# One RWKV-7 recurrence and squared-ReLU FFN on one core: the square taken from PSUM, early parts moved up, a solve's input loaded ahead, and one more group by seven products

## The chip, the cores and the metric

The kernel runs on one core of a Trainium2 chip. The metric is the device time of one execution in microseconds (us). The engines are named as in the profile: PE (TensorE, matrix products and transposes), DVE (VectorE), ACT (ScalarE), POOL (GpSimd) and SP (SyncE, which issues most DMAs). The time before is a median of 948.04 us over 3 runs (943.51 to 949.66).

## The reference

```python
# 4 batches, 8 heads, 768 steps, head size 40, one 40x40 state per head
for t in range(S):
    y[:, :, t] = einsum('bhd,bhde->bhe', r_t, state)
    Sa = einsum('bhde,bhe->bhd', state, a_t)
    state = state * w_t[:, :, None, :] - einsum('bhd,bhe->bhde', Sa, b_t)
    state = state + einsum('bhd,bhe->bhde', v_t, k_t)
x = y as 3072 rows of 320                    # 8 heads x 40
out = maximum(x @ w_in, 0)**2 @ w_out        # w_in 320 x 2048, w_out 2048 x 320
```

All of it is fp32. The two weight matrices arrive as the bits of float64 numbers and are turned into fp32 on the chip.

## The kernel before

**Chunks.** Time is cut into 24 chunks of 128 steps (4 batches of 6), and a chunk holds all 8 heads. Two chunks make a group of 256 rows for the FFN, so there are 12 groups, 0 to 11.

**The early part** of a chunk (`early`) needs nothing of the state: it transposes w, takes running products of the decays by scans on DVE (L372 to L381), transposes b and a, scales them (`bT` L387, `decay` L388) and forms the matrix N, which is stored to HBM (`kept_d` for the later chunks). `ahead` says in which slot which chunk's early part is made.

**The solves** invert triangular matrices made of N. POOL does them, a unit of chunks at a time, by 63 steps of a product (L478) and a subtraction (L480). Units of sizes 4, 4 and 2 end the list: chunks 14 to 17 (I call it unit 8), 18 to 21 (unit 9), 22 and 23 (unit 10). `take` loads a unit's N into the one buffer `half_n` on POOL's own DMA queue (L451); the result `half_t` is stored to `kept_t` (L487), and a later slot loads its chunk's inverse `T` from there, on SP's queue (L507).

**A slot** is the time in which chunk i's chain runs (state, `minus_x`, `xr`, and last `tokens`, L697), with the next chunk's inputs prepared (products masked into `RV`, `A`, `RX` at L347; `kvT` L548; `in_k`, `in_b` L588), one or two early parts, and FFN work between them. Slots 0 to 6 are laid out by hand as a string of words: in it `pa`/`pd` are the two halves of a piece of weight conversion (ACT L275; DVE L284 to L292), `th` and `wh` the FFN calls below, `sq` the square. Slots 7 to 23 come from `sorted_slot`. Nothing is reordered at run time: each engine works through its instructions in the order of these calls.

**The FFN** (class `Ffn`). A quad is a quarter of the hidden rows of a group; a group has four. `thirds` opens two PSUM banks of the pool `ps_f` (which has only two) with 4 products, `whole` adds 8 more, and ACT writes the relu to `hid` (L762), one operation a bank. `square` later multiplies `hid` by itself on DVE (L769). `make_quarter` adds a quad's share to one chunk's output by 4 products of 128x320; from group `SEVEN` = 6 on, `make_piece` instead makes a group's output by seven sums of 8 products of 128x160 each (P1 to P7), with sums of weight blocks made once (`sum_weights`) and sums of `hid` blocks (L825, L826). The profile shows every fp32 product as two records, so a quarter is a row x8 and a piece a row x16. The names `in_ab`, `in_w` and `decay` in the rows of the pieces are buffers that hold sums of weights by then.

Of the kernel before, what the change touches and what calls it, by code (L numbers as in the profile page):

```python
# [17 lines left out]
def kernel(  # L18
# [22 lines left out]
    nc = tc.nc  # L41
# [682 lines left out]
    class Ffn:  # L724
# [26 lines left out]
        def whole(self):  # L751
# [4 lines left out]
            for e, p_ in enumerate(self.banks):  # L756
# [5 lines left out]
                nc.scalar.activation(h_, p_.rearrange("p f t -> p (f t)"), Act.Relu)  # L762
                self.unsquared.append(h_)
# [3 lines left out]
        def square(self):  # L767
            for h_ in self.unsquared:
                nc.vector.tensor_tensor(h_, h_, h_, Alu.mult)  # L769
            self.squared += len(self.unsquared) // 2  # L770
            self.unsquared = []
# [25 lines left out]
        def make_piece(self, g, at):  # L797


            names = "P1 P4 P2 P7 P6 P5 P3" if g == len(order) // GB - 1 else "P4 P1 P2 P7 P6 P5 P3"  # L800
# [11 lines left out]
            if at in (0, 3, 4):  # L812
                self.bank = psum(ps_f)
# [5 lines left out]
            for n in range(NF // 2):  # L819
                k, e, m_ = n // 4, n // 2 % 2, n % 2  # L820
                mm(ps[part], x_[:, n], seven[name][k * QF + 2 * m_ + e], at in (0, 3, 4) and n == 0)
# [14 lines left out]
            if at == 3:  # L836
                plus(hi1, ps[0], hi0)
            if at == 6:
                plus(hi0, ps[2], hi0)
                plus(hi1, ps[0], hi1)  # L840
                plus(hi0, ps[0], hi0)
                less(lo1, hi1, lo1)
                plus(hi0, ps[1], hi0)
                plus(hi1, ps[1], hi1)
                for n, o_ in enumerate(self.ends):
                    bb, c = order[g * GB + n]
                    row = bb * S + c * C
                    store(out[row:row + C, :], o_, 2)
# [14 lines left out]
    SEVEN = 6  # L863
# [169 lines left out]
    ahead = {7: (14, 15), 8: (16, 17)}  # L1033
    ahead.update({i: (i + 9,) for i in range(9, len(order) - 9)})

    done = set(range(14))
    unit = len(solves)
# [26 lines left out]
    def sorted_slot(i, g, ch):  # L1064
# [4 lines left out]
        one, two = (made + [iter(()), iter(())])[:2]  # L1069
# [7 lines left out]

        if more and "x" in n:
# [6 lines left out]
        step(of(turn_rv), on(one), on(one))  # L1085
        fetch_next(j + 1, "r")
        step(second.make_quarter)
        step(on(ch), of(decay_state))
        if i == 2 * SEVEN + 3:
            sum_weights(0)  # L1090
        if i == 2 * SEVEN + 4:
            sum_weights(3)
        step(of(make_rv), second.thirds)
        step(on(ch), on(one))
        if fine:
            join()
        step(second.whole)
        step(on(ch))
        step(on(one), of(turn_k))
        if i == 2 * SEVEN + 3:  # L1100
            sum_weights(1)
# [67 lines left out]
```

## Time and profile before

| | |
|---|---|
| median of 3 runs (us) | 948.04 (943.51 to 949.66) |
| the profiled execution (us) | 944.9, of which the span is 943.2 |
| mean granted PE clock | 0.956 |
| PE busy | 883.6 us (94%) |
| DVE busy | 518.8 us (55%) |
| ACT busy | 283.0 us (30%) |
| POOL busy | 525.1 us (56%) |

The span runs from the first to the last instruction; the execution has 1.7 us around it. Rows below that start with a time are from the timeline or the chain of waits: start and duration in us from the start of the span, engine, line, operation, output<-input, and in brackets the idle time of that engine just before and what ended it. xN says that N instructions of the same kind are merged into the row; for PE the duration of the last one overlaps the next row.

### The profile page before, as it was taken

Reading aid. Unit: us, or ns where it says so; the run is one execution under the profiler, and the core shown is the slowest. Engines: PE = TensorE matmul, PEld = TensorE weight load, DVE = VectorE, ACT = ScalarE, POOL = GpSimd, SP = SyncE. Lnnn points to the kernel's source line nnn. Section 1 sums busy time; section 2 is a strip of 40 time slices with the busy share of each in tenths; the row PEclk is TensorE's granted clock in tenths of the full one; section 3 lists DMA queues with packets and bytes.
Section 4 is the critical chain, followed back from the end, with each engine's and each line's share of the span. In section 5 each row is a group of like instructions: output and inputs, shape, how many; then the busy total and the mean of one; then the engine's idle time right before and its main releaser. Section 6 shows DMA issues by size and latency. Waiting matters only on the chain.

```text
span 943.2 us, 23218 instructions
## 1 busy us (share of the span) xinstructions
PE 883.6 (94%) x9404; PEld 738.8 (78%) x9404; DVE 518.8 (55%) x1209; ACT 283.0 (30%) x735; POOL 525.1 (56%) x935
## 2 busy tenths in 40 slices
PE   6678989889999999999999999999989999999997
PEld 5466657667787887888888888888978999988897
DVE  5827657888853454553755454675634645343243
ACT  3033334544523333333333332222212222222110
POOL 4557347065007786418999959999958986000000
PEclk9858988799899999999999999999998999999999
DMA  9769779766866578987665776604355445040000
GB/s 110 127 145 143 171 136 180 184 160 129 178 101 154 93 128 161 170 163 131 126 92 87 127 178 113 115 17 86 57 131 93 74 81 99 18 75 1 22 15 15
DMA packets 253269, 103.41 MB, mean 110 GB/s; under 512 B 234154, under 2 KB 240298, under 8 KB 252010
## 3 DMA queue, kind: packets, MB, share of 16 engines
q1 hardware_dynamic: 244709, 83.00, 49.7%
q0 software_dynamic: 3760, 17.10, 7.4%
q10 hardware_dynamic: 4693, 1.83, 0.9%
q8 instruction: 74, 1.21, 0.6%
q14 instruction: 33, 0.27, 0.1%
HBM read 69.00 MB, written 30.92 MB: 106 GB/s over the span
## 4 chain that ended last, share of the span: by engine, by line
PE 47%; POOL 25%; DVE 11%; DMA 8%; issue 4%; ACT 3%; SPq 2%; ACTq 0%; DVEq 0%; POOLq 0%
PE ps_f L87 21%; POOL half_t L480 13%; POOL half_p L478 12%; PE ps_w L87 11%; PE ps_c L87 8%; PE ps_w L331 3%; DMA half_n<-kept_d 2%; PE ps_f L264 2%; DMA in_r<-in_r_dram 1%; DMA T<-kept_t 1%; SPq L513 1%; DVE half_t L480 1%; DVE half_t L478 1%; DVE decay L381 1%; DMA dec<-kept_e 1%
## 5 line engine op out<-in xcount | busy, mean ns | idle before, releaser
L478 POOL TENSOR_TENSOR half_p<-half_n,half_t 128x462 f32<-128x462 f32 (+39 forms) x406 | 229.2, 565 | 75.7 <-DMA half_n<-kept_q 23.7
L480 POOL TENSOR_TENSOR half_t<-half_t,half_p 128x462 f32<-128x462 f32 (+39 forms) x406 | 245.7, 605 | 31.8
L87 PE MATMUL ps_f<-w_out,hid 128*128 128x320 f32 (+1 forms) x768 | 165.4, 368 | 0.0
L87 PE MATMUL ps_f<-tokens,w_in 128*128 128x256 f32 x672 | 157.0, 387 | 0.0
L87 PEld LDWEIGHTS ps_f<-w_out,hid 128*128 128x128 f32 x768 | 123.2, 190 | 26.0
L87 PEld LDWEIGHTS ps_f<-tokens,w_in 128*128 128x128 f32 x672 | 125.9, 192 | 19.1 <-issue 2.0
L769 DVE TENSOR_TENSOR hid<-hid 128x512 f32<-128x512 f32 x96 | 82.3, 899 | 10.3 <-ACT hid L762 9.9
L762 ACT ACTIVATE hid<-ps_f 128x512 f32<-128x512 f32 x84 | 49.8, 596 | 80.9 <-PE ps_f L87 80.8
L372 DVE TENSOR_TENSOR_SCAN decay<-ps_w,ones 128x64 f32<-128x64 f32 x88 | 23.9, 271 | 66.1 <-PE ps_w L331 66.0
L451 POOL DMA_DIRECT2D half_n<-kept_q x18 | 9.5, 534 | 88.7 <-DMA kept_m<-N 26.4
L697 DVE TENSOR_TENSOR tokens<-ps_c,dec 128x512 f32<-128x512 f32 x24 | 16.6, 691 | 72.9 <-PE ps_c L87 71.1
L347 DVE TENSOR_TENSOR RX<-ps_w,upper 128x512 f32<-128x512 f32 x48 | 30.8, 684 | 38.4 <-PE ps_w L87 38.2
L87 PEld LDWEIGHTS ps_c<-xr,T 64*64 64x64 f32 x768 | 29.7, 146 | 25.2 <-issue 18.4
L264 PE MATMUL ps_f<-ident 128*128 128x512 f32 (+3 forms) x108 | 49.4, 591 | 0.0
L87 PE MATMUL ps_f<-tokens,w_third 64*128 64x256 f32 x336 | 47.6, 394 | 0.1
L398 ACT COPY N<-ps_w 128x256 f32<-128x256 f32 x48 | 17.7, 369 | 94.9 <-PE ps_w L87 67.7
L548 DVE TENSOR_TENSOR kvT<-ps_w,dec 128x512 f32<-128x512 f32 x24 | 16.4, 684 | 52.5 <-PE ps_w L331 23.3
L87 PE MATMUL ps_c<-xr,T 64*64 64x40 f32 x768 | 35.7, 240 | 10.1 <-DMA T<-kept_t 5.4
L347 DVE TENSOR_TENSOR RV<-ps_w,upper 128x512 f32<-128x512 f32 x48 | 30.9, 685 | 21.2 <-PE ps_w L87 20.9
L658 ACT COPY minus_x<-ps_c 64x160 f32<-64x160 f32 x96 | 27.5, 287 | 36.5 <-PE ps_c L87 32.6
L331 PE MATMUL ps_w<-ident,in_ab 128*128 128x128 f32 x184 | 28.5, 301 | 10.1 <-DVE RV L347 8.1
L87 PE MATMUL ps_w<-rT,kvT 40*128 40x128 f32 x384 | 31.4, 308 | 5.4 <-ACT kvT L561 5.1
(167 smaller groups left out, 1548.9 us busy)
## 6 DMA issues: line engine op xcount, KB each, us to landing
dec<-kept_e SPq DMA_DIRECT2D x22, 633.8 KB
kept_e<-decay SPq DMA_DIRECT2D x19, 633.8 KB
in_w<-in_w_dram SPq DMA_DIRECT2D x24, 160.0 KB
in_b<-in_b_dram SPq DMA_DIRECT2D x24, 160.0 KB
in_ab<-in_a_dram SPq DMA_DIRECT2D x24, 160.0 KB
in_r<-in_r_dram SPq DMA_DIRECT2D x24, 160.0 KB
in_v<-in_v_dram SPq DMA_DIRECT2D x24, 160.0 KB
in_k<-in_k_dram SPq DMA_DIRECT2D x22, 160.0 KB
```

What stands on the lines that cost most here:

```text
L87: nc.tensor.matmul(o, l_, r_, start=start, stop=True, skip_group_check=True)
L264: nc.tensor.matmul(fill_bank[:, :n * 128], ident, ident.unsqueeze(1).to_broadcast([128, n, 128]), start=True, stop=True, skip_group_check= ...
L331: nc.tensor.transpose(p_[:, q * 128:(q + 1) * 128], pair(x_, q), ident)
L347: nc.vector.tensor_tensor(t_, p_, over4(upper), Alu.mult)
L372: nc.vector.tensor_tensor_scan(up[:, q, MID + 1:C + 1], wT[:, q, MID:], ones, 1.0, Alu.mult, Alu.mult)
L398: nc.scalar.copy(plain, p_[:, ::2].rearrange("s h (f t) -> s f h t", f=2))
L478: eng.tensor_tensor(p_, part[:, at:at + m_].unsqueeze(1).to_broadcast([128, n, m_]), t3[:, :n, s:s + 1].to_broadcast([128, n, m_]), Alu.mult)
L480: eng.tensor_tensor(t3[:, :n, s + 1:], t3[:, :n, s + 1:], p_, Alu.subtract)
L658: nc.scalar.copy(flipped(xn)[halves[half], flip, :, :, :D], by_pair(xs[halves[half ^ flip]]))
L697: nc.vector.tensor_tensor(t_, y_, g["up"][:, :, :C], Alu.mult)
L762: nc.scalar.activation(h_, p_.rearrange("p f t -> p (f t)"), Act.Relu)
L769: nc.vector.tensor_tensor(h_, h_, h_, Alu.mult)
```

## The change

Five things are changed.

1. `whole` issues, right behind the two relus, one DVE operation each that reads the PSUM bank and the relu: max(PSUM, 0) x relu, written over `hid`. `square` keeps only its count. The operation so stands in DVE's order at the place of `whole` (L763 in the changed kernel) and no longer at that of `square`, and a PSUM bank of `ps_f` comes free after it.
2. `SEVEN` is 5: group 5 (chunks 10 and 11) is also made by seven products, and the weight sums are made two slots earlier (slots 13 and 14).
3. In the last group, P6's and P5's sums are added before the last product, from banks of another pool, and one half of the output is stored earlier.
4. `ahead`: slot 9 also makes two early parts (chunks 18 and 19), and chunks 20 to 23 follow one slot earlier than before. The parts are now issued at numbered places of the slot.
5. `solve_more`: the first 2048 of the 3072 words a row of the next unit's N are loaded once the unit before has passed step 40, the rest when that unit has ended.

```diff
@@ -760,13 +760,12 @@
                         mm(p_[:, n], w_in[:, j, f * 128:(f + 1) * 128], t_[:, j, :], False)
                 h_ = hidden[:, self.place(k), e]
                 nc.scalar.activation(h_, p_.rearrange("p f t -> p (f t)"), Act.Relu)
+                nc.vector.scalar_tensor_tensor(h_, p_.rearrange("p f t -> p (f t)"), 0.0, h_, Alu.max, Alu.mult)
                 self.unsquared.append(h_)
             self.banks = None
             self.quad += 1
 
         def square(self):
-            for h_ in self.unsquared:
-                nc.vector.tensor_tensor(h_, h_, h_, Alu.mult)
             self.squared += len(self.unsquared) // 2
             self.unsquared = []
 
 
-            names = "P1 P4 P2 P7 P6 P5 P3" if g == len(order) // GB - 1 else "P4 P1 P2 P7 P6 P5 P3"
+            last = g == len(order) // GB - 1
+            names = "P1 P4 P2 P7 P6 P5 P3" if last or g == SEVEN else "P4 P1 P2 P7 P6 P5 P3"
...
             half, chunk = {"P1": (0, 0), "P2": (1, 0), "P4": (1, 1), "P7": (0, 1), "P6": (0, 0), "P5": (1, 1), "P3": (1, 0)}[name]
             part = {"P1": 0, "P2": 2, "P4": 1, "P7": 0, "P6": 0, "P5": 1, "P3": 2}[name]
-            if at in (0, 3, 4):
-                self.bank = psum(ps_f)
+            fresh = at in ((0, 3, 4, 5, 6) if last else (0, 3, 4))
...
-                mm(ps[part], x_[:, n], seven[name][k * QF + 2 * m_ + e], at in (0, 3, 4) and n == 0)
+                mm(ps[part], x_[:, n], seven[name][k * QF + 2 * m_ + e], fresh and n == 0)
...
+            if at == 4:
+                self.sixth = ps[0]
+            if at == (4 if last else 6):
+                plus(hi1, self.sixth, hi1)
+                plus(hi0, self.sixth, hi0)
+                less(lo1, hi1, lo1)
+            if at == 5:
+                self.fifth = ps[1]
+            if at == (5 if last else 6):
+                plus(hi1, self.fifth, hi1)
+                plus(hi0, self.fifth, hi0)
             if at == 6:
                 plus(hi0, ps[2], hi0)
-                plus(hi1, ps[0], hi1)
-                plus(hi0, ps[0], hi0)
-                less(lo1, hi1, lo1)
-                plus(hi0, ps[1], hi0)
-                plus(hi1, ps[1], hi1)
-                for n, o_ in enumerate(self.ends):
-                    bb, c = order[g * GB + n]
-                    row = bb * S + c * C
-                    store(out[row:row + C, :], o_, 2)
+            for n in {5: (1,), 6: (0,)}.get(at, ()) if last else (1, 0) if at == 6 else ():
+                bb, c = order[g * GB + n]
+                row = bb * S + c * C
+                store(out[row:row + C, :], self.ends[n], 2)
             return True
 
         def rest(self):
...
-    SEVEN = 6
+    SEVEN = 5
...
 
-    ahead = {7: (14, 15), 8: (16, 17)}
-    ahead.update({i: (i + 9,) for i in range(9, len(order) - 9)})
+    ahead = {7: (14, 15), 8: (16, 17), 9: (18, 19), 10: (20,), 11: (21,), 12: (22,), 13: (23,)}
 
     done = set(range(14))
-    unit = len(solves)
+    under_way = [len(solves), None]
+
+    def solve_more():
+
+        u, now = under_way
+        while u < len(units) and all(m_ in done for m_ in range(len(order)) if unit_of[m_] == u):
+            flush()
+            take(u, own, slice(0, EARLIER))
+            if now is not None:
+                run(now)
+            take(u, own, slice(EARLIER, None))
+            now = solving(u, (40,))
+            next(now)
+            u += 1
+        if u == len(units) and now is not None:
+            run(now)
+            now = None
+        under_way[:] = u, now
...
-        one, two = (made + [iter(()), iter(())])[:2]
+        place = [0]
+
+        def at_place():
+            place[0] += 1
+            for gen, places in zip(made, ((1, 1, 5, 8, 10, 12), (9, 10, 11, 12, 13, 14) if i == 8 else (13, 14, 14, 14, 14, 15))):
+                for _ in range(places.count(place[0])):
+                    next(gen, None)
+
...
+        def sums(n_):
+            if i == 2 * SEVEN + 3 + (n_ > 0):
+                sum_weights(n_)
+
...
             join()
-        step(of(turn_rv), on(one), on(one))
+        step(of(turn_rv), at_place)
         fetch_next(j + 1, "r")
-        step(second.make_quarter)
-        step(on(ch), of(decay_state))
-        if i == 2 * SEVEN + 3:
-            sum_weights(0)
-        if i == 2 * SEVEN + 4:
-            sum_weights(3)
-        step(of(make_rv), second.thirds)
-        step(on(ch), on(one))
+        step(second.make_quarter, at_place)
+        step(on(ch), of(decay_state), at_place)
+        sums(0)
+        sums(1)
+        step(of(make_rv), second.thirds, at_place)
+        step(on(ch), at_place)
         if fine:
             join()
-        step(second.whole)
-        step(on(ch))
-        step(on(one), of(turn_k))
-        if i == 2 * SEVEN + 3:
-            sum_weights(1)
-        step(of(turn_down))
-        step(on(one), on(ch))
-        step(on(ch), of(scale_kb))
+        step(second.whole, at_place)
+        sums(3)
...
+        step(on(ch), of(make_a), second.thirds, at_place)
         fetch_next(j + 1, "v")
-        step(of(turn_state), second.square, second.whole, on(two))
-        if i == 2 * SEVEN + 3:
-            sum_weights(2)
+        step(of(turn_state), second.square, second.whole, at_place)
+        sums(2)
         if not early_join and not fine:
             join()
...
-        step(second.square, second.make_quarter, on(two), on(two))
-        if i in ahead and len(ahead[i]) > 1:
-            step(on(two), on(two))
-        step(second.make_quarter, on(two))
-        for gen in (one, two, joining):
+        step(second.square, second.make_quarter, at_place)
+        step(second.make_quarter, at_place)
+        for gen in made + [joining]:
...
         ch = g["chain"]
+        sorted_slot(i, g, ch)
         done.update(ahead.get(i, ()))
-        sorted_slot(i, g, ch)
-        while unit < len(units) and all(m_ in done for m_ in range(len(order)) if unit_of[m_] == unit):
-            flush()
-            take(unit, own)
-            solve(unit)
-            unit += 1
+        solve_more()
```

What moves on the engines is shown at three places.

DVE, slot 4 of the part laid out by hand: the wholes of the first two quads of group 0, between the masked `RV` and the second half of the early part of chunk 8 (`decay_126`). L284 to L292 are a piece of weight conversion. Before:

```order
L347 TENSOR_TENSOR RV<-ps_w,upper 128x512 x2
L284 SCALAR_TENSOR_TENSOR hid<-hid 128x320
L285 SCALAR_TENSOR_TENSOR w_out<-w_out,hid 128x320
L290 TENSOR_SCALAR hid<-hid 128x320
L291 TENSOR_TENSOR w_out<-hid,w_out 128x320
L292 TENSOR_SCALAR hid<-hid 128x320
L377 RECIPROCAL decay_126<-decay_126 128x4
L378 RECIPROCAL decay_126<-decay_126 128x4
```

and after:

```order
L347 TENSOR_TENSOR RV<-ps_w,upper 128x512 x2
L763 SCALAR_TENSOR_TENSOR hid<-ps_f,hid 128x512 x2
L284 SCALAR_TENSOR_TENSOR hid<-hid 128x320
L285 SCALAR_TENSOR_TENSOR w_out<-w_out,hid 128x320
L290 TENSOR_SCALAR hid<-hid 128x320
L291 TENSOR_TENSOR w_out<-hid,w_out 128x320
L292 TENSOR_SCALAR hid<-hid 128x320
L763 SCALAR_TENSOR_TENSOR hid<-ps_f,hid 128x512 x2
L377 RECIPROCAL decay_126<-decay_126 128x4
L378 RECIPROCAL decay_126<-decay_126 128x4
```

Two pairs of squares now stand ahead of the reciprocals; before, all eight squares of this group stood behind the next masked `A`, further down.

DVE, slot 8, which makes a second early part (`decay_127`) as the next chunk's `in_k`, `in_b` and `RX` are prepared. Before:

```order
L387 TENSOR_TENSOR bT<-ps_w,decay_126 128x512
L388 TENSOR_TENSOR decay_126<-ps_w,decay_126 128x4x128
L588 TENSOR_TENSOR in_k_107<-ps_w,in_k_107 128x8x40
L588 TENSOR_TENSOR in_b_87<-ps_w,in_b_87 128x8x40
L347 TENSOR_TENSOR RX<-ps_w,upper 128x512 x2
```

and after (eight scans of `decay_127` stand between `decay` L388 and the first row, and six more behind the last):

```order
L373 SCALAR_TENSOR_TENSOR decay_127<-ps_w,ones 128x64
L588 TENSOR_TENSOR in_k_107<-ps_w,in_k_107 128x8x40
L588 TENSOR_TENSOR in_b_87<-ps_w,in_b_87 128x8x40
L377 RECIPROCAL decay_127<-decay_127 128x4
L378 RECIPROCAL decay_127<-decay_127 128x4
L380 SCALAR_TENSOR_TENSOR decay_127<-ps_w,decay_127,ones 128x63
L381 SCALAR_TENSOR_TENSOR decay_127<-ps_w,decay_127,ones 128x63
```

The sixteen scans and two reciprocals of the second early part come ahead of `RX`; before they came after `tokens`, at the end of the slot.

POOL, from step 40 of unit 8 on; `kept_d_220` is the N of unit 9. The difference at step 40:

```order
 L478 TENSOR_TENSOR half_p<-half_n,half_t 128x480
 L480 TENSOR_TENSOR half_t<-half_t,half_p 128x20x24
+L451 DMA half_n<-kept_d_220 64x2048 x2
 L478 TENSOR_TENSOR half_p<-half_n,half_t 128x483
 L480 TENSOR_TENSOR half_t<-half_t,half_p 128x21x23
```

and at the end of that unit:

```order
 L480 TENSOR_TENSOR half_t<-half_t,half_p 128x32
 L487 DMA kept_t_230<-half_t 128x2048
-L451 DMA half_n<-kept_d_220 64x3072 x2
+L451 DMA half_n<-kept_d_220 64x1024 x2
 L467 MEMSET half_t 128x2048
 L469 MEMSET half_t 64x32 x2
```

Two thirds of the load of unit 9 now stand ahead of the last 23 steps of unit 8. The load waits for the stores of chunks 18 to 21, and these 23 steps stand behind it on POOL.

More of the change, by code (lines that the diff above doesn't have):

```diff
@@ L811, in make_piece @@
             part = {"P1": 0, "P2": 2, "P4": 1, "P7": 0, "P6": 0, "P5": 1, "P3": 2}[name]
-            if at in (0, 3, 4):
-                self.bank = psum(ps_f)
+            fresh = at in ((0, 3, 4, 5, 6) if last else (0, 3, 4))
+            if fresh:
+                self.bank = psum(ps_w if at > 4 else ps_f)
             if at == 0:
@@ L1084, in sorted_slot @@
             join()
-        step(of(turn_rv), on(one), on(one))
+        step(of(turn_rv), at_place)
         fetch_next(j + 1, "r")
-        step(second.make_quarter)
-        step(on(ch), of(decay_state))
-        if i == 2 * SEVEN + 3:
-            sum_weights(0)
-        if i == 2 * SEVEN + 4:
-            sum_weights(3)
-        step(of(make_rv), second.thirds)
-        step(on(ch), on(one))
+        step(second.make_quarter, at_place)
[4 more added lines that the diff above has]
+        step(on(ch), at_place)
         if fine:
             join()
-        step(second.whole)
-        step(on(ch))
-        step(on(one), of(turn_k))
-        if i == 2 * SEVEN + 3:
-            sum_weights(1)
-        step(of(turn_down))
-        step(on(one), on(ch))
-        step(on(ch), of(scale_kb))
+        step(second.whole, at_place)
+        sums(3)
+        step(on(ch), at_place)
+        step(at_place, of(turn_k))
+        step(of(turn_down), at_place)
+        step(at_place, on(ch))
+        step(on(ch), of(scale_kb), at_place)
         if fine:
             join()
-        step(on(ch), of(make_a), second.thirds, on(one))
+        step(on(ch), of(make_a), second.thirds, at_place)
         fetch_next(j + 1, "v")
-        step(of(turn_state), second.square, second.whole, on(two))
-        if i == 2 * SEVEN + 3:
-            sum_weights(2)
+        step(of(turn_state), second.square, second.whole, at_place)
+        sums(2)
         if not early_join and not fine:
```

## The prediction

> **What bounds the kernel now.** I read the page first (its busy shares and the chain that ended last), then who waited for whom on PE, then PE's clock by windows, and last the timeline around the waits.
>
> ```profile
> PE 883.6 (94%) x9404; PEld 738.8 (78%) x9404; DVE 518.8 (55%) x1209; ACT 283.0 (30%) x735; POOL 525.1 (56%) x935
> PE 47%; POOL 25%; DVE 11%; DMA 8%; issue 4%; ACT 3%; SPq 2%; ACTq 0%; DVEq 0%; POOLq 0%
> ```
>
> PE is busy in 94% of the span, so a microsecond is won only by less PE work or by a PE wait that goes. POOL's 25% of the chain says that one stretch is timed by the solves. The waits of PE from 380 us on, who waited <- for whom, us in total, times, longest:
>
> ```profile
> PE ps_c L87 <- DMA T<-kept_t: 5.4, 1, 5.4
> PE ps_w L87 <- DVE decay L388: 0.4, 1, 0.4
> ```
>
> From 380 us to the end there is one large wait, in slot 17, for unit 9's inverse. All else there is PE work. The columns of the next rows are busy us of PE, PEld, DVE, ACT and POOL, then the granted PE clock:
>
> ```profile
> 220.00:230.00 10.00, 9.04 (x92) 7.38 (x92) 6.33 (x14) 4.14 (x12) 5.83 (x18) 1.00 0.56 142
> 250.00:260.00 10.00, 10.00 (x61) 7.89 (x59) 8.99 (x27) 4.25 (x10) 1.05 (x2) 0.70 0.86 146
> 700.00:725.00 25.00, 19.64 (x183) 17.11 (x183) 8.78 (x20) 5.16 (x12) 15.09 (x37) 0.86 0.78 144
> ```
>
> The 5.36 us in which PE pauses after 703 are the missing busy time of the last row, and its clock falls to 0.86 behind them.
>
> **The solves (ahead, solve_more).** POOL's rows, with the load of unit 8, its first step, its step 40, its end, and the same for unit 9:
>
> ```profile
> 415.18 1.04 POOL L451 DMA_DIRECT2D half_n<-kept_d  x2 [25.14 <-DMA kept_d<-N]
> 426.77 0.58 POOL L478 TENSOR_TENSOR half_p<-half_n,half_t 128x63 f32<-128x63 f32 x1 [8.34 <-DMA half_n<-kept_d]
> 508.83 1.22 POOL L480 TENSOR_TENSOR half_t<-half_t,half_p 128x480 f32<-128x480 f32 x1
> 549.91 0.60 POOL L487 DMA_DIRECT2D kept_t<-half_t  x1 [0.30 <-POOL half_t L480]
> 554.84 1.81 POOL L467 MEMSET half_t<- 128x2048 f32 x1 [3.15 <-DMA kept_t<-half_t]
> 562.26 0.36 POOL L478 TENSOR_TENSOR half_p<-half_n,half_t 128x63 f32<-128x63 f32 x1 [5.20 <-DMA half_n<-kept_d]
> 693.76 5.14 DMA kept_t<-half_t
> 699.56 8.85 DMA T<-kept_t
> 490.58 0.34 SPq L110 DMA_DIRECT2D kept_e<-decay  x1
> 496.49 1.82 SPq L110 DMA_DIRECT2D kept_d<-N  x4
> ```
>
> Unit 8's load takes 426.77 - 415.18 = 11.6 us. Loading two thirds of the words before the first step leaves about 2/3 x 11.6 = 7.7, and chunk 17's early part now ends some 2 us sooner in slot 8 (one FFN quarter, 2.25 us by the next part, now comes behind it instead of before; an estimate). So its first step stands near 421, 5.6 us earlier, and step 40 near 503. There POOL's queue has to wait for chunk 21's stores. The last two rows are chunk 20's, in slot 11; chunk 21 takes that slot now, and slot 9's second early part pushes it back by some 2.4 us of PE (its 16 products take 1.16, the row at 367.27 below, its transpositions I count the same), so the four stores are issued until 496.49 + 1.82 + 2.4 = 500.7 and land a few us later, about 503 too. Queued behind this wait are unit 8's last 23 steps. I count 0 for it; 3 us of it would still be harmless. Unit 8 then ends 5.6 us earlier, near 544.3, and unit 9 starts when its memset is done rather than its load: 554.84 + 1.81 + 0.1 - 5.6 = 551.2 instead of 562.26. The remaining third of the load (11.6/3 = 3.9 us) is hidden by the store and the memset. All later steps of unit 9 move by 11 us, and the inverse lands at 708.4 - 11 = 697.4. PE asks for it at 703.2 now, at about 701 without the 2.2 us of the next part. The wait goes with some 3.5 us to spare. The half speed behind it goes too; the first rows of each pair are behind the wait, the second in slot 7 for the same work:
>
> ```profile
> 708.54 1.08 PE L87 MATMUL ps_c<-xr,T 64*64 64x40 f32 x16 [5.36 <-DMA T<-kept_t]
> 709.55 2.08 PE L87 MATMUL ps_w<-rT,kvT 40*128 40x128 f32 x16
> 711.42 1.92 PE L87 MATMUL ps_f<-tokens,w_third 64*128 64x256 f32 x8
> 337.06 0.66 PE L87 MATMUL ps_c<-xr,T 64*64 64x40 f32 x16
> 337.65 1.16 PE L87 MATMUL ps_w<-rT,kvT 40*128 40x128 f32 x16
> 338.64 1.03 PE L87 MATMUL ps_f<-tokens,w_third 64*128 64x256 f32 x8
> ```
>
> That is 5.36 + 0.42 + 0.92 + 0.89 = **-7.6 us**. Next late would be unit 10's inverse, whose solve moves forward as well.
>
> **Seven products for group 5.** Two quarters (x16 rows of 128x320) and two pieces (x32 rows of 128x160):
>
> ```profile
> 283.99 4.57 PE L87 MATMUL ps_f<-w_out,hid 128*128 128x320 f32 x16
> 697.80 4.51 PE L87 MATMUL ps_f<-w_out,hid 128*128 128x160 f32 x32
> ```
>
> A quarter and a piece cost about 2.25 us each (the next rows begin 4.5 us on). Eight become seven: **-2.2 us**. The weight sums move from slots 15 and 16 to 13 and 14, where DVE is idle as often; I count them at nothing, since their cover, an idle DVE, is the same, and half a microsecond if it is not.
>
> **The tail.** The first of the six last adds and the last store:
>
> ```profile
> 938.44 0.33 DVE L825 TENSOR_TENSOR o<-ps_f,o 128x160 f32<-128x160 f32 x1 [6.19 <-PE ps_f L87]
> 940.11 0.42 SPq L110 DMA_DIRECT2D out_dram<-in_w  x1
> ```
>
> One add stays behind the last product, so the last store is issued at 938.8 instead of 940.11: **-1.3 us**.
>
> **The square at its new place.** In bulk it is free: DVE has 45% idle. What counts is where an in-order DVE now stands behind a relu while PE waits for what comes next. The first such place is slot 4, where PE waits for DVE:
>
> ```profile
> 209.14 1.25 ACT L762 ACTIVATE hid<-ps_f 128x512 f32<-128x512 f32 x2
> 211.58 1.27 DVE L347 TENSOR_TENSOR RV<-ps_w,upper 128x512 f32<-128x512 f32 x2
> 211.68 1.13 PE L87 MATMUL ps_f<-tokens,w_third 64*128 64x256 f32 x8
> 212.75 3.72 PE L87 MATMUL ps_f<-tokens,w_in 128*128 128x256 f32 x16
> 215.56 0.17 DVE L377 RECIPROCAL decay<-decay 128x4 f32<-128x4 f32 x1
> 217.30 1.09 ACT L762 ACTIVATE hid<-ps_f 128x512 f32<-128x512 f32 x2
> 221.10 1.55 PE L87 MATMUL ps_w<-rT,xnT 40*128 40x128 f32 x15 [0.59 <-DVE bT L387]
> ```
>
> Before, relu freed the two banks at 210.4 and the next quad's thirds started at 211.68. Now the first pair of squares stands behind `RV` and takes as long as it (1.27, the same shape from PSUM), until 214.1. The thirds start 2.4 us later, the whole ends at 216.5 + 2.2 = 218.7, the two relus at about 219.3 and 219.8, the second pair of squares at 220.4. The reciprocals, 215.56 before, wait for it: 4.8 us. Everything to `bT` follows, and PE already waits there (0.59), so it is **+4.8 us** on the path. Its bounds are 1.3 (the first pair alone) and 8 (with PE's clock halved for 6 us behind it).
>
> Three smaller places. In slot 6 the next quad's thirds need the bank that the relu at 313.84 frees; behind it now stands one operation more, of 0.7 as the rows of L347 show: **+0.7**. Slot 7: a pair of squares (1.27) goes ahead of `kvT` and `in_b`, whose PSUM banks PE needs again soon; between 0 and 1.27 I take **+0.6**. Slot 8: the second early part's scans and reciprocals now stand ahead of `RX`.
>
> ```profile
> 313.84 0.60 ACT L762 ACTIVATE hid<-ps_f 128x512 f32<-128x512 f32 x1 [1.07 <-PE ps_f L87]
> 367.27 1.16 PE L87 MATMUL ps_w<-decay,bT 40*128 40x128 f32 x16 [0.44 <-DVE decay L388]
> 398.88 0.29 DVE L372 TENSOR_TENSOR_SCAN decay<-ps_w,ones 128x64 f32<-128x64 f32 x1
> 402.39 0.33 DVE L381 TENSOR_TENSOR_SCAN decay<-ps_w,decay,ones 128x63 f32<-128x63 f32 x1
> ```
>
> The last two rows are the first and the last of those 18 operations, as they ran at the end of that slot: 3.8 us. PE can hide part of that behind its thirds (about 1 us) and `minus_x`; between 0 and 3.8 I take **+2.0**. In return the squares that stood ahead of the scans at the end of slots 7 and 8 no longer delay PE, 0.44 us each (the row at 367.27, and the second row of the waits above): **-0.9**.
>
> [...] These rows, of squares (two SBUF operands) and of a masked product from PSUM, give min/median/max in ns:
>
> ```profile
> L769 DVE TENSOR_TENSOR hid<-hid x24: 681/685/693, 812.7 to 925.3; 128x512 f32<-128x512 f32 x24
> L347 DVE TENSOR_TENSOR RX<-ps_w,upper x6: 681/686/692, 810.3 to 866.5; 128x512 f32<-128x512 f32 x6
> ```
>
> Both take the same, so I add nothing.
>
> **The sum.** -7.6 - 2.2 - 1.3 - 0.9 = -12.0; +4.8 + 0.7 + 0.6 + 2.0 = +8.1; together -3.9 against the profiled execution of 944.9, whose span is 943.2 with 1.7 around it. That execution lies 1.6 under the mean of the four shown (943.51, 944.9, 948.04, 949.66: 946.5). I forecast **942.6**.
>
> **The rivals.**
> A, the gains land and the new order costs little. For it: DVE idles nearly half the time, and the rows behind a pause show PE catching up with nothing else late. Then slot 4 costs its lower bound, 1.3, and the rest 0.7: 946.5 - 12.0 + 2.0 = 936.5.
> B, the inverse stays late. POOL now stops at step 40 behind chunk 21's stores, and its steps stand behind that stop. It decides once unit 9 ends more than 3.5 us later than I have it; at 9 us the whole wait is back: 942.6 + 7.6 = 950.2. Against it: the stop and the stores meet near 503 by two separate sums.
> C, slower: pauses of PE draw half speed. The window at 250 has clock 0.70 behind a stretch in which PE paused only briefly, and slot 17's has 0.86. If the 4.8 us in slot 4 and the 2.0 in slot 8 do the same, at 25 x 0.14 = 3.5 us each and twice in slot 4, it gives 942.6 + 10.5 = 953.1. [...]
>
> **How the numbers follow.** Forecast 0.46 (938 to 947 by itself: slot 4 and slot 8 between their bounds), A 0.28, B 0.12, C 0.14. About 1% (9.5 us) is what a measurement of this kernel tells from no change. Faster by more, under 938.6: three quarters of A and a fifth of the forecast, 0.21 + 0.09 = 0.30. Slower by more, over 957.5: half of C, where slots 7 and 9 pause too, 0.07, and B and C together, 0.02: 0.09. The rest, 0.61, is the same. A range of 933 to 953 leaves out a tenth of A's lower end and the upper half of C with the tail of B.
>
> **What would show it.** Right: no PE wait on `T<-kept_t`, unit 9's first step near 551 + the shift of slots before, a PE clock of 1.00 from 700 to 725; seven x16 rows in group 5; one add behind the last product; and in slot 4 a PE wait of some 4 to 5 us on `bT` or the scans, with DVE idle for ACT's relu before L763. Wrong: POOL idle at step 40 for more than 4 us (B); clock under 0.9 around 220 or 390 (C); or `bT` in slot 4 as early as before (A). If PE's own work grew, by slower products for instance, none of the cases holds.

## The result, and the profile after

The changed kernel takes 958.86 us (median of 6 runs, 952.3 to 964.98) against 947.3 us for the kernel before on the same chip (943.51 to 949.66): a ratio of 1.0138 [1.0101, 1.0174]. It is 1.4% slower, outside the range. The profiled execution took 953.66 us, one of its quicker ones (the one before: 944.9), so its trace shows 8.8 us of a loss of 11.6 by the medians and 13 by the ratio. Ratios below are to runs of the kernel before on the experiment's own chip, with their 95% intervals; they leave out executions more than 1.5% above the fastest of their kernel, which are three of the ten of e9 and one of the ten of e6.

The busy shares and the chain that ended last, after:

```profile
PE 883.2 (93%) x9452; PEld 741.2 (78%) x9452; DVE 508.1 (53%) x1221; ACT 282.3 (30%) x735; POOL 511.8 (54%) x943
PE 73%; DVE 10%; DMA 6%; ACT 4%; issue 3%; POOL 1%; SPq 1%; ACTq 0%; POOLq 0%; DVEq 0%
```

PE is busy as long as before, though group 5's products should take 2.2 us less of it. POOL's part of the chain fell from 25% to 1%: the solves time nothing any more. Yet the time is longer, so PE stands idle, or runs slower, in other places. By windows from the start of slot 4 to the end of slot 17 it does both: it idles 23.2 us instead of 10.7, and is busy 7.9 us longer. A table by slot finds the places. A slot's length here is the time between the starts of successive `tokens` (L697) in the timeline; what a slot does behind its `tokens` counts with the next, and "tail" is from the last one to the end of the span. The four right columns are experiments told below; the trace of e2 is of the slowest of its ten executions (959.9 us, their median 952.19).

| slots (us) | before | after | old square (e1) | square alone (e2) | new from slot 7 (e10) | new to slot 6 (e11) |
|---|---|---|---|---|---|---|
| 0-3 | 189.85 | 186.94 | 189.45 | 192.36 | 190.66 | 187.16 |
| 4 | 47.69 | 53.40 | 47.99 | 55.43 | 47.48 | 55.86 |
| 5 | 29.39 | 29.37 | 27.81 | 28.17 | 29.38 | 28.18 |
| 6 | 56.34 | 57.07 | 56.34 | 57.07 | 56.35 | 57.07 |
| 7 | 36.13 | 40.14 | 35.61 | 38.74 | 37.49 | 38.45 |
| 8-9 | 73.34 | 78.39 | 84.21 | 82.06 | 81.40 | 85.74 |
| 10-13 | 135.57 | 137.47 | 138.88 | 135.50 | 137.46 | 138.96 |
| 14-17 | 125.23 | 128.22 | 123.13 | 126.20 | 128.21 | 125.69 |
| 18 | 35.82 | 28.49 | 28.48 | 28.49 | 28.49 | 28.49 |
| 19-23 | 142.93 | 142.94 | 142.94 | 142.93 | 142.93 | 142.94 |
| tail | 70.91 | 69.48 | 69.46 | 70.85 | 69.45 | 69.47 |

Slot 18 gives 7.33 back and the tail 1.43, as forecast. By the end of slot 17 PE is 17.5 us behind the kernel before (711.0 against 693.54), where the forecast's terms made +5.0. Slots 0 to 3 show how far single traces differ by themselves: no kernel here differs there from the one before, and in the sixteen traces they take 186.9 to 192.4.

**Slot 4.** The timeline of DVE and then PE, after:

```profile
211.44 1.27 DVE L763 SCALAR_TENSOR_TENSOR hid<-ps_f,hid 128x512 f32<-128x512 f32 x2
217.60 1.30 DVE L763 SCALAR_TENSOR_TENSOR hid<-ps_f,hid 128x512 f32<-128x512 f32 x2 [2.29 <-ACT hid L762]
218.82 0.17 DVE L377 RECIPROCAL decay<-decay 128x4 f32<-128x4 f32 x1
212.16 1.73 PE L87 MATMUL ps_f<-tokens,w_third 64*128 64x256 f32 x8 [0.76 <-DVE hid L763]
213.82 3.72 PE L87 MATMUL ps_f<-tokens,w_in 128*128 128x256 f32 x16
221.10 0.66 PE L582 MATMUL ps_w<-ident,dec 128*128 128x128 f32 x4 [1.82 <-DVE decay L381]
```

This is the order that the prediction described. The thirds wait for the first square, DVE waits 2.29 for the second pair's relu, and only then come the reciprocals. `RV` starts 1.34 earlier than before (210.24 for 211.58); measured from it, the reciprocals are 218.82 + 1.34 - 215.56 = 4.6 later. PE waits for the scans behind them.

**Slot 7.** Its start, all engines, and SP's load that follows:

```profile
326.78 0.69 DVE L697 TENSOR_TENSOR tokens<-ps_c,dec 128x512 f32<-128x512 f32 x1 [1.80 <-PE ps_f L87]
328.06 1.29 DVE L763 SCALAR_TENSOR_TENSOR hid<-ps_f,hid 128x512 f32<-128x512 f32 x2
328.86 2.39 PE L87 MATMUL ps_f<-w_out,hid 128*128 128x320 f32 x8 [1.68 <-issue]
334.62 1.32 SPq L513 DMA_DIRECT2D blocks<-kept_t  x2
348.81 0.30 DVE L570 TENSOR_TENSOR f<-end,dec 128x4 f32<-128x4 f32 x1 [6.82 <-DMA dec<-kept_e]
```

Slot 6's last quad has its squares queued behind `tokens`, for which DVE first waits 1.80. The quarter on PE needs a bank of `ps_f`, which now comes free only after the first square, at 328.75, and PE stands for 1.68 (the profile names no releaser; in the kernel before, where ACT frees the bank, the same products begin at 323.51, 0.24 after `tokens` and without a wait, here 2.08 after it; in e3 below, where ACT frees it too, the wait is gone). The next load is issued 334.62 - 326.78 = 7.84 after `tokens`; before it was 5.93 (329.20 - 323.27). And `dec`, from behind it in SP's queue, comes later still: `f` starts 22.0 after `tokens`, and 18.6 before.

**Slot 17 and 18: the inverse.** The timeline: the first step of unit 8, its stop at step 40, its end, unit 9's first step, the load of `T` and the product that uses it. Then the windows, with PE's clock in the one quoted of before:

```profile
435.64 0.29 POOL L478 TENSOR_TENSOR half_p<-half_n,half_t 128x63 f32<-128x63 f32 x1 [5.85 <-DMA half_n<-kept_d]
514.83 1.08 POOL L451 DMA_DIRECT2D half_n<-kept_d  x2
554.13 0.60 POOL L487 DMA_DIRECT2D kept_t<-half_t  x1 [0.30 <-POOL half_t L480]
562.54 1.51 POOL L478 TENSOR_TENSOR half_p<-half_n,half_t 128x63 f32<-128x63 f32 x1
697.78 1.68 SPq L507 DMA_DIRECT2D T<-kept_t  x2
720.57 0.66 PE L87 MATMUL ps_c<-xr,T 64*64 64x40 f32 x16
```

```profile
700.00:725.00 25.00, 24.87 (x309) 22.86 (x308) 9.71 (x22) 5.50 (x14) 21.55 (x45) 1.00 0.33 60
```

The wait on `T` is gone and the clock is 1.00 instead of 0.86. But unit 9 begins at 562.54, where it began before (562.26), and its `T` is fetched 1.1 us earlier (697.78 for 698.92). PE asks for it at 720.57, 17 us later than the 703.2 of before. The wait went because PE came late.

### The profile page after: what moved, and what is told of

It is laid out like the page before. It is cut to its first block, busy times and chain, and to the rows that moved or that the text cites. A ratio compares the mean times of both kernels' runs of the same rounds, so it can differ in the third digit from the quotient of the medians.

```text
span 951.9 us, 23327 instructions
## 1 busy us (share of the span) xinstructions
PE 883.2 (93%) x9452; PEld 741.2 (78%) x9452; DVE 508.1 (53%) x1221; ACT 282.3 (30%) x735; POOL 511.8 (54%) x943
## 4 chain that ended last, share of the span: by engine, by line
PE 73%; DVE 10%; DMA 6%; ACT 4%; issue 3%; POOL 1%; SPq 1%; ACTq 0%; POOLq 0%; DVEq 0%
PE ps_f L87 36%; PE ps_w L87 15%; PE ps_c L87 12%; PE ps_w L331 5%; DMA dec<-kept_e 2%; PE ps_f L264 1%; PE ps_c L598 1%; PE ps_c L671 1%; DMA kept_q<-N 1%; PE ps_w L582 1%; DMA half_n<-kept_q 1%; DMA in_w<-in_w_dram 1%; DVE hid L763 1%; POOL half_t L480 1%; POOL half_p L478 1%
## 5 line engine op out<-in xcount | busy, mean ns | idle before, releaser
L480 POOL TENSOR_TENSOR half_t<-half_t,half_p 128x462 f32<-128x462 f32 (+39 forms) x406 | 237.0, 584 | 31.8
L478 POOL TENSOR_TENSOR half_p<-half_n,half_t 128x462 f32<-128x462 f32 (+39 forms) x406 | 221.0, 544 | 59.7 <-DMA half_n<-kept_q 22.7
L87 PE MATMUL ps_f<-w_out,hid 128*128 128x160 f32 (+1 forms) x736 | 152.4, 360 | 1.7 <-issue 1.7
L87 PEld LDWEIGHTS ps_f<-w_out,hid 128*128 128x128 f32 x736 | 115.8, 190 | 23.4 <-issue 1.9
L763 DVE SCALAR_TENSOR_TENSOR hid<-ps_f,hid 128x512 f32<-128x512 f32 x84 | 57.2, 688 | 108.2 <-ACT hid L762 108.2
L87 PE MATMUL ps_f<-tokens,w_third 64*128 64x256 f32 x336 | 51.6, 407 | 1.5 <-DVE hid L763 1.5
L347 DVE TENSOR_TENSOR RV<-ps_w,upper 128x512 f32<-128x512 f32 x48 | 30.9, 685 | 17.3 <-PE ps_w L87 17.0
L87 PEld LDWEIGHTS ps_f<-tokens,w_third 64*128 64x128 f32 x336 | 34.3, 199 | 5.7 <-DVE hid L763 2.7
L87 PE MATMUL ps_f<-decay,hid 128*128 128x160 f32 x224 | 33.3, 302 | 1.6 <-DVE hid L827 1.6
```

The costliest lines, as they stand in the source:

```text
L87: nc.tensor.matmul(o, l_, r_, start=start, stop=True, skip_group_check=True)
L347: nc.vector.tensor_tensor(t_, p_, over4(upper), Alu.mult)
L478: eng.tensor_tensor(p_, part[:, at:at + m_].unsqueeze(1).to_broadcast([128, n, m_]), t3[:, :n, s:s + 1].to_broadcast([128, n, m_]), Alu.mult)
L480: eng.tensor_tensor(t3[:, :n, s + 1:], t3[:, :n, s + 1:], p_, Alu.subtract)
L763: nc.vector.scalar_tensor_tensor(h_, p_.rearrange("p f t -> p (f t)"), 0.0, h_, Alu.max, Alu.mult)
```

## The experiments

The theory with which they began: the square at its new place costs more than the forecast's +8.1, and the other four parts bring what was forecast. Its rivals: the other parts lose (the earlier solves, the earlier loads or the weight sums); or it is the PSUM form of the square that loses, by the bank it holds, and not its place in DVE's order.

**Which part: the old square with everything else (e1), and the new square alone (e2).** e1 is the changed kernel with

```diff
-                nc.vector.scalar_tensor_tensor(h_, p_.rearrange("p f t -> p (f t)"), 0.0, h_, Alu.max, Alu.mult)
...
         def square(self):
+            for h_ in self.unsquared:
+                nc.vector.tensor_tensor(h_, h_, h_, Alu.mult)
```

> The kernel after with the square as before (two SBUF operands, issued at the old call, so that ACT's relu frees the PSUM bank); everything else as after. Place theory (the new square costs where DVE, in order, stands behind a relu: 5.7 us in slot 4, 0.7 in slot 6, about 4 in slot 7): 958.9 - 10.4 = about 948, and PE's pause behind RV in slot 4 as short as before. Rival, that the early parts, the sums and the loads lose it all: stays within 3 us of 958.9.

Measured: 944.91 us, 0.9987 [0.996, 1.0014]. e2 is the same edit the other way round, in the kernel before.

> The kernel before with the new square alone. Place theory: 947.3 + 10.4 = about 957 (slot 7's part may be less, since its late dec load has other causes too: then 954). Rival: within 3 us of 947.3.

Measured: 952.19 us, 1.0071 [1.0038, 1.0104]. So the square is the part that loses: with it, the four other parts go from 0.9987 to 1.0138, some 14 us (0.0151 of 945). Alone it loses 6.7 us, but in e2 too slot 18 is 28.49: the late PE no longer waits for the inverse, though no load is made ahead. Some 7 us of the same loss are hidden there by a wait that would have been anyway.

The other parts bring nothing to speak of. In e1's profile slot 18 and the tail gain 8.8, and slots 8 and 9 lose 10.9. PE in slot 8 of e1, and below it SP's queue and PE there in the changed kernel:

```profile
388.66 1.09 PE L331 MATMUL ps_w<-ident,in_w 128*128 128x128 f32 x4 [6.59 <-DMA in_w<-in_w_dram]
```

```profile
384.19 4.58 SPq L110 DMA_DIRECT2D kept_d<-N  x4
389.43 0.58 SPq L146 DMA_DIRECT2D in_w<-in_w_dram  x1
392.97 0.63 PE L331 MATMUL ps_w<-ident,in_w 128*128 128x128 f32 x4 [1.81 <-DMA in_w<-in_w_dram]
```

The second early part of slot 8 now starts at step 9 of the slot instead of its end, and its `in_w` isn't there yet: its load stands in SP's queue behind four stores of N that take 4.58 to issue. Behind the wait PE's clock falls, here in a window of the changed kernel (the clock stands third from the end):

```profile
398.00:402.00 4.00, 3.82 (x32) 3.58 (x34) 2.59 (x5) 0.00 (x0) 0.00 (x0) 0.60 0.83 197
```

Over slots 8 and 9 PE has 896 records both before and after the change, and is busy 75.5 us for them instead of 72.5. Yet the moved part is not the only way to lose here. e2, whose slot 8 is as before, loses 8.7 in these two slots: PE waits 4.05 in slot 9, through ACT for the load of `blocks`, and runs at 0.50 behind it (435 to 445).

**Place or form: the square behind its relu, but from SBUF (e3).**

```diff
-                nc.vector.scalar_tensor_tensor(h_, p_.rearrange("p f t -> p (f t)"), 0.0, h_, Alu.max, Alu.mult)
+                nc.vector.tensor_tensor(h_, h_, h_, Alu.mult)
```

> The kernel after with the square at its new place, right behind the relu, but as hid x hid from SBUF, so that ACT's relu and not DVE frees the PSUM bank. If the order of DVE costs: slot 4 keeps about 4 of its 5.7 us, the waits of thirds and quarters for a bank (0.7 and 1.7) go: about 955. If the late bank costs: slot 4 loses its price too, about 948.

Measured: 964.64 us, 1.0203 [1.0152, 1.0255]. Here ACT frees the banks again, and it doesn't help: slot 4 is 55.37. Only slot 6 returns to 56.34, so its 0.73 was the bank. The place in DVE's order is the loss. The whole is slower than either value expected; in the trace 9.4 us of it stand in slots 10 to 13 (146.88, against 137.47 in the changed kernel), and why is open. The PSUM form is the better of the two, as the groups show (x count | busy us, mean ns | idle before); after, and e3:

```profile
L763 DVE SCALAR_TENSOR_TENSOR hid<-ps_f,hid 128x512 f32<-128x512 f32 x84 | 57.2, 688 | 108.2 <-ACT hid L762 108.2
```

```profile
L763 DVE TENSOR_TENSOR hid<-hid 128x512 f32<-128x512 f32 x96 | 76.4, 803 | 134.9 <-ACT hid L762 134.6
```

**Which squares: new only from slot 7 (e10), only in slots 0 to 6 (e11).**

```diff
-                nc.vector.scalar_tensor_tensor(h_, p_.rearrange("p f t -> p (f t)"), 0.0, h_, Alu.max, Alu.mult)
+                if not opening[0]:
+                    nc.vector.scalar_tensor_tensor(h_, p_.rearrange("p f t -> p (f t)"), 0.0, h_, Alu.max, Alu.mult)
```

for e10, `if opening[0]:` for e11 (true in the slots laid out by hand), and the old square for the others.

> The kernel after with the old square in the part laid out by hand (slots 0 to 6) and the new one from slot 7 on. In the profiles slot 4 took about 6.7 us more with the new square and slot 6 took 0.7 more. If these places carry the price: 958.9 - 7.4 = 951.5 (ratio 1.006). If the later slots carry it: 957 or more.

> The other half: the new square in slots 0 to 6, the old one from slot 7 on. By the same reading 944.9 + 7.4 = 952.3 (ratio 1.0066); if the later slots carry the price: 946 or less.

Measured: e10 946.19 us, 1.0029 [0.9994, 1.0064]; e11 959.62 us, 1.0177 [1.015, 1.0205]. The 16 squares (8 quads) in the slots laid out by hand hold the whole loss; the 80 behind them cost 0.0042 against e1, which is as wide as its interval (0.0044, from the two). The price is more than twice the 7.4 expected: 0.0190 against e1, some 18 us. Of the 13.7 that e11's trace shows against e1's, 7.9 are in slot 4, 0.7 in slot 6 and 2.8 in slot 7. The pair also shows what delays the load in slot 7. `tokens` and this load, in e10 and in e11:

```profile
323.87 0.69 DVE L697 TENSOR_TENSOR tokens<-ps_c,dec 128x512 f32<-128x512 f32 x1 [1.80 <-PE ps_f L87]
329.80 1.32 SPq L513 DMA_DIRECT2D blocks<-kept_t  x2
```

```profile
328.27 0.69 DVE L697 TENSOR_TENSOR tokens<-ps_c,dec 128x512 f32<-128x512 f32 x1 [1.80 <-PE ps_f L87]
330.34 2.39 PE L87 MATMUL ps_f<-w_out,hid 128*128 128x320 f32 x8 [1.68 <-issue]
336.11 1.32 SPq L513 DMA_DIRECT2D blocks<-kept_t  x2
```

5.93 and 7.84: it is the squares of slot 6 that delay this load, by 1.9, and not slot 7's own. Slot 7's own squares cost as well: the slot takes 37.49 in e10 with these alone, 38.45 in e11 with slot 6's alone, and 35.6 to 36.3 in the eight traces with neither.

**The two pairs of slot 4: old for these alone (e14), new for these alone (e15).** The condition above becomes `k >= 2` and `k < 2`, k being the quad's number.

> The kernel after with the old square for the first two quads of group 0 alone (the pair behind RV and the pair ahead of the reciprocals in slot 4). In ten profiles slot 4 took 47.5 to 48.9 us with the old square there and 52.7 to 55.9 with the new one. If these two places are that difference: slot 4 back at 48, and 958.9 - 6.5 = 952.4 (ratio 1.007); if the later squares of the part laid out by hand share it: slot 4 at 50 or more.

> The reverse: the new square for these two quads alone, the old one for all others (ratio 0.9987 without any new square). If the two places cost their 6.5 us whatever comes later: 944.9 + 6.5 = 951.4 (ratio 1.006), slot 4 near 54.6, slots 6 and 7 as with the old square (56.3 and about 36). If the price of the squares in slots 0 to 6 (1.9% by the two halves) is all here: 960.

Measured: e14 953.04 us, 1.0108 [1.0039, 1.0176]; e15 951.47 us, 1.0068 [1.0034, 1.0102]. Put into e1, these four operations cost 0.0068 + 0.0013 = 0.8%, some 7.7 us. Taken out of the changed kernel they give 0.3%, within the intervals: what is gained there is partly lost again, slots 8 and 9 of e14 taking 84.8 against 78.4. In the profiles, slot 4 takes 52.7 to 56.5 in the seven kernels that have these pairs at the new place, and 47.5 to 49.3 in the nine that have them at the old one; the means are 54.9 and 48.3, apart by 6.6. Why more than the 4.6 of the changed kernel's trace? PE in slot 4 of e15, and its windows:

```profile
211.30 2.67 PE L87 MATMUL ps_f<-tokens,w_third 64*128 64x256 f32 x8 [1.80 <-DVE hid L764]
213.90 6.03 PE L87 MATMUL ps_f<-tokens,w_in 128*128 128x256 f32 x16
223.49 0.66 PE L582 MATMUL ps_w<-ident,dec 128*128 128x128 f32 x4 [1.82 <-DVE decay L381]
```

```profile
210.00:215.00 5.00, 3.70 (x11) 2.39 (x12) 4.38 (x9) 0.94 (x4) 4.30 (x10) 0.68 0.90 112
215.00:220.00 5.00, 5.00 (x18) 4.08 (x17) 0.69 (x1) 1.68 (x6) 4.14 (x12) 0.64 0.00 0
```

The same products as at 212.16 and 213.82 above take 0.94 + 2.31 = 3.25 longer, at a clock of 0.68 and 0.64 where the changed kernel's trace has 1.00 in both windows. In e11 they run at 0.66 from 210 to 215. In these traces the lower clock stands behind the longer pauses: PE waits 1.40, 1.42 and 1.80 ahead of these thirds in e11, e7 and e15, which have the lower clock behind it, and 0.76, 0.55 and not at all in the changed kernel, e2 and e12, which keep 1.00. From `RV` to the reciprocals it is 8.6 us in the latter three, 10.2 to 11.8 in the former, and 3.8 to 4.7 with the old pairs. From `bT` to the end of the slot, at clocks of 0.83 to 0.91, six of the seven traces with the new pairs lose 1.6 to 3.2 more against the 17.3 of the changed kernel and of seven of the nine with the old.

**The other parts one by one.** e5 is e1 with `SEVEN = 6`, so without the seventh products of group 5, and the weight sums at the corresponding later slots.

> The kernel after with the old square and with seven products from group 6 on as before, so that only the early parts, the loads ahead and the tail are left of the change. Theory: the wait for unit 9's inverse is gone (-7.3) and the tail shorter (-1.4), slot 8's new order costs up to 5: 943 to 947. Rival, that the early parts' order is what loses: 952 or more.

Measured: 951.3 us, 1.0065 [1.0033, 1.0097]. Group 5 by seven products is thus worth 0.8% in e1's surroundings, more than the 2.2 us forecast; but the sums also stand elsewhere in e5 (its slot 16 takes 36.20, against 29.82 in e1), so this isn't the price of the products alone. The time lies near the rival's 952, and slots 8 and 9 of e5 take 80.31 (before: 73.34).

The weight sums have a price where their slot is late. DVE and PE in slot 14 of the changed kernel, and a window of it:

```profile
596.68 0.27 DVE L570 TENSOR_TENSOR f<-end,dec 128x4 f32<-128x4 f32 x1 [12.64 <-DMA dec<-kept_e]
598.36 2.29 DVE L886 TENSOR_TENSOR decay<-decay,w_out 128x1280 f32<-128x1280 f32 x1
603.08 2.12 DVE L892 TENSOR_TENSOR w_out<-w_out 128x1280 f32<-128x1280 f32 x1
605.13 0.68 DVE L548 TENSOR_TENSOR kvT<-ps_w,dec 128x512 f32<-128x512 f32 x1
608.37 1.91 PE L87 MATMUL ps_f<-tokens,w_third 64*128 64x256 f32 x7
```

```profile
605.00:610.00 5.00, 4.08 (x32) 3.21 (x28) 4.09 (x8) 0.00 (x0) 4.69 (x5) 0.70 0.01 3
```

DVE idles 12.64 for `dec`, then makes the sums, and `kvT`, which PE needs, stands behind them. e6 (on e1) and e7 (on the changed kernel) move the sums ahead of that wait:

```diff
+        sums(1)
+        sums(2)
         step(second.make_quarter)
...
         step(second.make_quarter, at_place)
+        sums(3)
```

with the same calls taken out further down.

> Old square as in the first experiment (944.9, ratio 0.9987), and three of the four sums of weights moved from between DVE's late work of slot 14 to the start of that slot, where DVE idles for 12 us. If sums behind the late dec load cost PE: tokens of slots 14 to 17 took 123.1 us there and 125.2 - 2.2 - 2.4 = 120.6 are due, so 2.5 us go: about 942.5. If an idle DVE covers them wherever they stand, as predicted: 944.9.

> The kernel after with the same move of three sums, new square kept. In the profile of after, slots 14 to 17 took 128.2 us and 120.6 are due: up to 7.6 us go, about 951.5, and PE's clock there stays at 1.00. If the sums are covered: 958.9.

Measured: e6 946.6 us, 1.0023 [0.9979, 1.0067]; e7 956.69 us, 1.0126 [1.0079, 1.0174]. In e7's profile slot 14 takes 30.31 instead of 36.41; in the time neither shows a gain that is clear of the intervals.

e8 (on e1) puts slot 8's second early part back to the end of the slot, and e9 takes both:

```diff
-            for gen, places in zip(made, ((1, 1, 5, 8, 10, 12), (9, 10, 11, 12, 13, 14) if i == 8 else (13, 14, 14, 14, 14, 15))):
+            for gen, places in zip(made, ((1, 1, 5, 8, 10, 12), (13, 14, 14, 14, 14, 15))):
```

> Old square, and the second early part of slot 8 issued at the end of the slot, as slots 7 and 9 have it. Slots 7 to 9 took 119.8 us in the profile of the first experiment and 109.5 before, of which PE waited 6.6 for in_w of that part. If its early place (its load too, behind 4.6 us of stores on SP's queue) costs PE: 940 or less. If that wait was chance: 944.9.

> Old square, sums at the start of slot 14, second early part of slot 8 at the end of the slot. If all three places are what turned the change's gains into a loss, the gains are left: -7.3 (unit 9's inverse), -2.2 (group 5), -1.4 (tail): 945.3 - 10.9 = about 934.5. If something else of the change costs too: 938 or more.

Measured: e8 944.79 us, 0.9987 [0.9958, 1.0016]. The wait for `in_w` is gone from slot 8, and slot 9 has one in its place (the ACT operation that PE waits for waits in turn for the load of `blocks`):

```profile
415.49 1.35 SPq L513 DMA_DIRECT2D blocks<-kept_t  x2
416.48 2.04 POOL L451 DMA_DIRECT2D half_n<-kept_d  x4 [26.15 <-DMA kept_d<-N]
422.69 0.91 ACT L522 ACTIVATE T<-blocks,which 128x256 f32<-128x256 f32 x2 [6.64 <-DMA blocks<-kept_t]
424.93 0.86 PE L671 MATMUL ps_c<-ident,minus_x 128*128 128x128 f32 x4 [3.44 <-ACT minus_x L658]
```

The upper rows show a second load near it, POOL's load of unit 8's N. In the sixteen traces the two go together. In the six in which POOL issues its load 1.13 us or more after SP begins to issue `blocks`, ACT uses `blocks` 3.3 to 4.7 us after that beginning; in the ten with 1.12 or less it is 6.6 to 10.7. No run moves one of the two loads alone, so the cause isn't shown, but it is a candidate for the waits in slot 9.

e9: 940.55 us, 0.9927 [0.9899, 0.9956], the one version whose ratio lies below both kernels. It is nearer the second expectation: something else of the change costs too. Its ten times fall into two groups, 933 to 941 and 951 to 954 us, and the trace is one of the second; the median of all ten (940.55) is 0.995 of the 945.24 of the kernel before. Neither half gains alone, and why the two gain together isn't shown. The trace of e9 takes 85.70 in slots 8 and 9, with a wait of 5.60 at the place of the last row above, where that of e13 below, the same but for the loads ahead, has no such wait and takes 73.78.

**The loads ahead: taken out of the changed kernel (e12) and out of e9 (e13).** The loop of `solve_more` becomes `flush(); take(u, own); solve(u); u += 1`, as before the change.

> The kernel after with each unit's input loaded whole when the unit before has ended, as before; the early parts stay a slot earlier. With the new square PE comes to slot 17 some 17 us later than before, and even with unit 9's inverse 11 us later it would be there in time. If so the loads ahead are worth nothing in this kernel: 958.9, and no wait of PE for the inverse. If they made the gain of slot 17: 958.9 + 7 = 966.

> The version with the old square, early sums and slot 8's second part at the end (ratio 0.9927), without the loads ahead. PE comes to slot 17 earlier there, so the wait for the inverse should be back in part: 940.6 + 2 to 9 = 943 to 949, and PE waits for it in the profile. If the loads are worth nothing anywhere: 940.6.

Measured: e12 954.62 us, 1.0119 [1.0079, 1.0159]; e13 947.2 us, 1.0036 [1.0009, 1.0064]. In the changed kernel they are worth nothing, and slot 18 is 28.49 without them. In e9 they are worth 0.9% (from the median of all ten times of e9) to 1.1% (from the ratios), some 8 to 10 us. PE's waits from 380 us on in e13 begin with

```profile
PE ps_c L87 <- DMA T<-kept_t: 9.1, 1, 9.1
```

so there the wait is back, since PE, at the end of slot 17 by 689.67, is early. Yet POOL's rows show that loads ahead have a price of their own, the stop at step 40. In the profiled execution of e9:

```profile
515.71 1.08 POOL L451 DMA_DIRECT2D half_n<-kept_d  x2 [5.37 <-DMA kept_d<-N]
```

It is 3.72 in e1 and nothing in the changed kernel (the row at 514.83 above has no wait).

## Why the prediction was wrong

Rival C (slower, by a lower clock behind pauses, 953.1) came nearest, and the forecast of 942.6 failed on both sides of its sum. The square's terms (4.8 + 0.7 + 0.6 - 0.9) made +5.2 and cost 14.3 by e1; the other four parts (-7.6 - 2.2 - 1.3 + 2.0) made -9.1 and brought 1.2, which is within the interval of e1.

**Slot 4, +4.8.** The mechanism held to the row: thirds behind the first square, DVE waiting for the second relu, reciprocals 4.6 later in the changed kernel's trace, against 4.8. Over the profiles the slot differs by 6.6, inside the bounds of 1.3 and 8, and in the timed runs the four operations cost 7.7, give or take 4. What the sum had left to rival C, the lower clock behind a pause, is the rest in most traces: 3.25 ahead of the reciprocals in e15, and up to 3.2 behind `bT` in others. Ahead of the reciprocals it stands behind pauses of 1.40 to 1.80 (e11, e7, e15).

**Slot 6, +0.7** was 0.73, and e3 shows that it was the bank. **Slot 7, +0.6** was 4.0 in the trace. The step looked at the slot's own squares, ahead of `kvT` and `in_b`. These cost 1.4 in e10's trace (37.49 for 36.13), and the larger part comes from the squares of the slot before, behind `tokens`, whose wait for PE they share: 1.68 on PE and 1.9 on SP's queue (e11), and 2.8 in the length of the slot against e1.

**Slot 8, +2.0 less 0.9.** Slots 8 and 9 lose 5.05. The step counted DVE's scans, and left out the loads that the moved part needs: `in_w` wasn't there, 1.81 in the changed kernel and 6.59 in e1, where PE comes sooner. It also left the lower clock to rival C: 2.0 of the 5.05 are idle PE, and 3.1 are the slower PE behind it (C had 3.5, and its sign, a clock under 0.9 around 390, comes soon after: 0.60 from 398 to 402). The 0.9 came: no wait of PE on `decay` L388 is left in these slots. In e1's trace this stretch alone takes the 8.8 that slot 18 and the tail win, so the parts without the square gain nothing (0.9987).

**Group 5, -2.2, sums at nothing.** Slots 10 to 17 should have been 2.2 shorter and are 4.9 longer. The extra early part of slot 9 only moves work between them. The cover named for the sums, an idle DVE, was not there: DVE idles in slot 14 for a late load, and the sums come behind it, ahead of `kvT`. Moving them mends the slot (e7) without a measured gain, so how much of the loss this is, and what makes the rest, stays open.

**Unit 9's inverse, -7.6** was -7.33, by another way. The first step of unit 8 was to be at 421 and is at 435.64, since its load waits for chunk 17's early part and PE was 7.5 late by then; the load took 10.1, not 7.7. Unit 9 was to begin near 551 and began at 562.54. Between the end of unit 8 and this step 8.4 us are left of 12.35, a gain of 3.9, not 5.4. By itself this would have left the inverse late, as rival B had it, and B's stop at step 40, counted 0 in the sum, is 3.72 in e1 and 5.37 in e9. But PE came later still. A wait that goes because the waiter is late is no gain: e2 and e12 lose it too, without the loads ahead. **The tail, -1.3**, is -1.4 in every kernel that has the edit (69.42 to 69.54 for 70.91).

**The square in bulk, and its form.** The four squares' own duration was right (688 ns from PSUM, 681 to 693 forecast). Over the whole kernel before, the old square took 899 in the mean (L769, 82.3 us busy), so the PSUM form does take work off DVE, but no run shows a gain from it at the later places (e10, 0.0042 slower than e1, within the interval).

**Open.** The trace of the changed kernel is one of its quicker executions and lacks 5 us of the median's loss; the lower clock in slot 4 would be some 3 of it (3.25 in e15), but no trace of that kernel shows it there. Why e9 falls into two groups of times is open as well; the order of the two loads in slot 9 is a candidate that no run tests.

## What to carry to other kernels

An operation that is put right behind another engine's result, on an engine that works in order, makes everything queued behind it wait for that result (in slot 4 DVE waits 2.29 for the relu, and the reciprocals come 4.6 later): cost it by its neighbours there, also across the border of the next stage, and by the buffer that it now holds. A wait that a delay hides can't be booked as a gain beside the delay: ask which of two chains (here PE's and POOL's) arrives last, after both have been moved. And before work is moved earlier, look up when each of its loads is issued.

## What the runs showed of the hardware

A lower clock stands behind some short pauses and not behind others. Behind one pause of 1.80 PE runs at 0.68 and 0.64 (e15, 210 to 220), and behind a pause of 1.82 later in the same slot it keeps 1.00 (e15, 220 to 225), so the length of one pause doesn't decide alone. And in the changed kernel the window from 605 to 610 has 0.70 with less than a microsecond of idle PE in it (5.00 - 4.08) and none in the ten before it, the thirds taking 1.91 for 7 records instead of 1.03 for 8.

DVE's square with both operands in SBUF takes longer in stretches in which POOL works. Its mean is 803 (e3) and 899 ns (before), where the same shape from PSUM takes 688. In the kernel before, from 440 to 700, where POOL is busy for 230.08 of the 260 us, it takes 681/1324/1680 ns (min/median/max). Where POOL is idle (0.00 from 810 to 930, the row of L769 in the prediction) the median is 685. From PSUM, in the changed kernel, it takes 651/692/693 from 440 to 700, with POOL busy for 233.36. POOL's products and subtractions take less time as well in the changed kernel, where DVE's square reads PSUM. They went from 229.2 + 245.7 us to

```profile
L480 POOL TENSOR_TENSOR half_t<-half_t,half_p 128x462 f32<-128x462 f32 (+39 forms) x406 | 237.0, 584 | 31.8
L478 POOL TENSOR_TENSOR half_p<-half_n,half_t 128x462 f32<-128x462 f32 (+39 forms) x406 | 221.0, 544 | 59.7 <-DMA half_n<-kept_q 22.7
```

From its first step to its store, unit 9 takes POOL 130.48 us there (562.54 to 693.02), 131.50 before (562.26 to 693.76) and 135.08 in e1 (561.60 to 696.68), which differs from the changed kernel in the square alone. Whether the square's form or its place gives POOL the time isn't shown by these.
